# Token sums, norm transpose and placing between the first and second pair of a fused convolution and SwiGLU kernel: a change of places

## The chip, the cores and the metric

The kernel runs on one core of a Trainium2 chip. The metric is the device time of one execution in microseconds (us). The profiled execution was recorded by the hardware profiler; "the trace" is that record. Engines are named as the profile does: PE is TensorE (PEld its weight loads), DVE is VectorE, ACT is ScalarE, POOL is GpSimd, and SP is SyncE, which here only issues DMAs.

## The reference

A causal convolution over the tokens, with seven taps per head, is followed by a feed-forward block: RMS norm, two projections from 192 to 1536, SiLU of one times the other, and a projection back to 192. All is float32.

```python
# convolution: B=8, S=4096, D=192, 8 heads of 24 channels, K=7 taps
w = softmax(weight, axis=-1)
x_pad = concatenate([zeros(K - 1 tokens), x], axis=1)
x = einsum('hk,bskhg->bshg', w, x_unf)          # x_unf: windows of x_pad
# feed-forward: 32768 tokens, 192 -> 1536 -> 192
xn = x / sqrt(mean(x * x, axis=-1) + 1e-06) * rms_g
g, val = xn @ w_gate, xn @ w_val
out = (g * sigmoid(g) * val) @ w_out
```

## The kernel before

The 32768 tokens are cut into 32 "pairs" of 1024 tokens, each two groups of 512. A pair's normalised tokens lie channel by channel in the tile xb (two groups, three blocks of 64 channels; the lower 64 partitions serve the gate half, the upper 64 the value half).

**The first pair** is computed plainly: L1012 makes the projections, L1052 the output product (function outer, L1045). Its output product collects two token blocks in each of two PSUM banks, one for either half of the array. ScalarE copies the lower bank to o_sb (function low, L1060), then VectorE adds the upper bank to it (function upp, L1064) and so frees the upper bank. This happens four times: twice for each group of tokens. L1069 stores a finished group.

**All later pairs** use a scheme with fewer products: instead of eight products of blocks it makes seven, and pays with sums of blocks. For the input side those are the token sums (x_sum, L667 to L671, eleven for each pair, listed in XSUM at L67: target, and two operands, of which 0 to 5 are blocks of xb and 6 to 15 are earlier sums in the tile xc) and weight sums made once (w_sums, L342). Products (L760) add up in PSUM banks, and ScalarE and VectorE copy and add banks between them. For the output side the weight sums are made once by GpSimd (out_sums, L823 to L829, twelve small subtractions of L826), and the output products are L900.

There are eight banks, ps0 to ps7; the first four are for the lower half of the array, the others for the upper. The second pair's products run in a fixed order. The first two of them write ps2 and ps6, then ps1 and ps7 (the fourth product waits for the upp that frees ps7), then ps0 and ps4 (the sixth waits for the last upp, which frees ps4), then ps2 and ps6 again, then ps3 and ps5, which ScalarE fills with copies of ps1 and ps7 before.

**The work ahead.** While a pair is multiplied, the tokens of a pair two places later are convolved and normalised. The norm has five steps (norm, L512): square on ScalarE (L461), reduce on VectorE (L472 to L474), factor on GpSimd (L478, L481 and two copies L484: the power -1/2 and its spreading over heads), spread on VectorE (L491, a transpose), and scale on GpSimd (L499, 128x1536). place (L623) writes the result to DRAM through eight DMAs on SyncE's queue (L636), from where fetch reads it back channel by channel into xb. load (L154) brings raw tokens, also through SyncE's queue.

**What sets the order.** In the steady state a list written out by hand (ORDER, L90) does, from the second pair on. Up to there a queue of due times does: put(at, do) at L695 enters a call under a number, and emit (L698) makes the calls in the order of their numbers; equal numbers go in the order of entry. The numbers are in units of the planner, not in us, and only their order counts. Each engine executes what it is given in that order, and waits where its input or its buffer isn't ready. base is the number at which the first pair's output product begins, and c is base + 200. From function outer the four upp lie at base + 1763, base + 1988, base + 2888 and base + 3788 (one pair of output products is 37.5). All calls in this queue come before ORDER begins, so the second pair's first products follow the first pair's last output products directly.

In the code before, the third pair's norm (pair number 2 in the code, counted from 0) stands at L1200, its placing at L1201, the second pair's eleven token sums at L1202 to L1205, and out_sums at L1206:

- reduce: base + 1800; factor: base + 2510; spread: base + 2620; scale: base + 2640; place: base + 2650
- the first seven token sums: base + 1860 to base + 2490; the eighth (number 10 of XSUM): base + 2560; the last three (numbers 8, 9, 4): base + 2895, 2900, 2905
- out_sums: twelve steps, base + 2600, 2660, and so on in steps of 60

Of the kernel before, what the change touches and what calls it, by code (L numbers as in the profile page):

```python
# [19 lines left out]
def kernel(  # L20
# [310 lines left out]
    def part(at, m, n):  # L331
        return spare[:, at : at + m * n].rearrange("p (m n) -> p m n", m=m)
# [179 lines left out]
    def norm(p):  # L512
        for part in (square, reduce, factor, spread, scale):
            part(p)
            yield
# [107 lines left out]
    def place(p):  # L623

        if p >= PAIRS:
            return
        y = yn.pop(p)  # L630
        xd = scr[p] = dram.tile([D, PT], F32, name="xd")
        to = xd[:].rearrange("(h a) (b t) -> h b a t", a=GS, t=TB)
        for first in range(2) if p == 1 else (0,):
            q = nc.scalar if first else nc.sync
            for h in range(first, H, 2 if p == 1 else 1):
                q.dma_start(out=to[h], in_=y[h::H])  # L636
            yield
# [57 lines left out]
    def put(at, do):  # L695
        heapq.heappush(line, (at, next(tick), do))
# [480 lines left out]
    def later(it, *places):  # L1177
        for at in places:
            put(at, functools.partial(next, it, None))

    base = NU * SPAN
# [6 lines left out]
    c = base + 200  # L1188
# [8 lines left out]
            at = c + 250 + 100 * k + 50 * j if j < 2 else c + 960 + 80 * k  # L1197
            put(at, functools.partial(part_tap, 2, k, j))
    put(base + 3900, functools.partial(load, 3))
    later(norm(2), c + 1510, c + 1600, c + 2310, c + 2420, c + 2440)  # L1200
    later(place(2), c + 2450)  # L1201
    xat = [c + i for i in (1660, 1730, 2060, 2130, 2200, 2270, 2290)]  # L1202
    xat += [c + 2360] + [base + i for i in (2895, 2900, 2905)]
    for i, at in zip((0, 1, 7, 2, 3, 5, 6, 10, 8, 9, 4), xat):
        put(at, functools.partial(x_sum, i))  # L1205
    later(out_sums(), *[base + 2600 + 60 * i for i in range(4 * NM)])  # L1206
# [49 lines left out]
```

## Time and profile before

| | us |
|---|---|
| three runs | 2610.17, 2610.87, 2611.08 |
| median | 2610.87 |
| the profiled execution's own time | 2610.16 |
| its span in the trace | 2608.0 |
| last output product of the first pair (L1052) ends | 134.59 |
| first product of the second pair (L760) | 133.79 |
| second pair's output products (L900) begin | 194.01 |
| third pair's products (L760) begin | 221.45 |

The mean granted clock of TensorE is 0.997 of full speed. The span is the time from the first to the last recorded work; 2.2 us of the execution's time lie around it. In a timeline, one line is a group of like instructions on one engine: start and length in us, engine, line of the code, operation, output and input tiles (with buffer numbers left out), how many, and in brackets the idle time before and what ended it. A product of L760 is recorded as two matmuls on one half of the array (64 of 128 rows), so a pair's 120 products are 240 records; two products, one on either half, run side by side.

### The profile page before, as it was taken

How to read it: one execution, taken by the hardware profiler on the slowest of the kernel's cores; microseconds unless marked ns; L12 is line 12 of the kernel's file. 1: busy time of each engine (PE TensorE's matmuls, PEld its weight loads, DVE VectorE, ACT ScalarE, POOL GpSimd, SP SyncE). 2: the span in 40 equal slices, each digit the busy share in tenths (PEclk: the TensorE clock that was granted, in tenths of full speed). 3: DMA queues.
4: the chain of work that ended last, by engine and by line, in shares of the span. 5: the costliest groups of instructions: out<-in, count | busy, mean ns of one | idle time of the engine just before them, and what ended most of it. 6: DMA issues, size and time to landing. Idle time of an engine off the chain costs nothing.

```text
span 2608.0 us, 60632 instructions
## 1 busy us (share of the span) xinstructions
PE 2573.4 (99%) x23794; PEld 1760.1 (67%) x23794; DVE 2318.2 (89%) x3679; ACT 1545.5 (59%) x2812; POOL 2190.9 (84%) x1786
## 2 busy tenths in 40 slices
PE   6999999999999999999999999999999999999999
PEld 3766667666676666676676766666766666766666
DVE  8989989889989889998899898898898998988975
ACT  5365556765556655557655566555576555676554
POOL 3888889888898888898888988888988888988877
PEclk9999999999999999999999999999999999999999
DMA  6212331223322223313133222233132332122220
GB/s 144 57 33 56 63 54 41 54 42 63 63 44 50 44 52 63 57 41 59 33 63 63 46 48 44 51 63 63 38 56 34 62 63 53 42 52 44 50 44 13
DMA packets 512635, 137.35 MB, mean 53 GB/s; under 512 B 484317, under 2 KB 486877, under 8 KB 512222
## 3 DMA queue, kind: packets, MB, share of 16 engines
q1 hardware_dynamic: 509100, 132.80, 26.8%
q8 instruction: 186, 3.05, 0.5%
q10 hardware_dynamic: 3248, 0.69, 0.1%
q14 instruction: 101, 0.82, 0.1%
HBM read 83.87 MB, written 49.55 MB: 51 GB/s over the span
## 4 chain that ended last, share of the span: by engine, by line
PE 97%; DVE 1%; POOL 1%; DMA 0%; issue 0%; ACT 0%; SPq 0%; DVEq 0%; POOLq 0%; ACTq 0%
PE ps L760 62%; PE ps L900 33%; PE ps L1012 2%; POOL wf L350 1%; DMA x<-in_x_dram 0%; DVE y L406 0%; DVE y L394 0%; PE ps L595 0%; DVE xc L304 0%; ACT xb L615 0%; DVE xc L671 0%; DVE ht L1029 0%; POOL yn L499 0%; POOL wf L346 0%; DVE y L389 0%
## 5 line engine op out<-in xcount | busy, mean ns | idle before, releaser
L760 PE MATMUL ps<-xc,wf 64*128 64x512 f32 x4960 | 1219.0, 592 | 0.0
L760 PEld LDWEIGHTS ps<-xc,wf 64*128 64x128 f32 x4960 | 681.4, 187 | 378.8 <-issue 185.0
L760 PE MATMUL ps<-xb,wf 64*128 64x512 f32 x2480 | 683.0, 591 | 4.4 <-DVE o_sb L1064 4.4
L709 ACT ACTIVATE tile<-ps 128x512 f32<-128x512 f32 x678 | 391.2, 593 | 396.6 <-PE ps L760 303.0
L709 ACT ACTIVATE tls<-ps 128x512 f32<-128x512 f32 (+1 forms) x562 | 323.5, 589 | 437.4 <-PE ps L760 220.9
L812 POOL TENSOR_TENSOR ht<-ht,tile 128x512 f32<-128x512 f32 x329 | 419.1, 1275 | 148.3 <-ACT tile L805 65.6
L760 PEld LDWEIGHTS ps<-xb,wf 64*128 64x128 f32 x2480 | 354.8, 187 | 187.2 <-issue 96.2
L812 POOL TENSOR_TENSOR ht<-ht,tls 128x512 f32<-128x512 f32 x260 | 330.8, 1274 | 86.1 <-ACT tls L805 42.1
L709 ACT ACTIVATE ps<-ps 128x512 f32<-128x512 f32 (+1 forms) x589 | 336.1, 580 | 88.6 <-PE ps L900 32.5
L928 POOL TENSOR_TENSOR early<-ht 128x512 f32<-128x512 f32 x279 | 354.9, 1276 | 5.1 <-POOL ht L812 0.3
L445 DVE SCALAR_TENSOR_TENSOR ps<-xh,tp,ps 128x512 f32<-128x512 f32 x450 | 320.6, 749 | 2.7 <-ACT ps L437 0.5
L900 PE MATMUL ps<-ht,wo_sb 128*32 128x128 f32 (+2 forms) x5208 | 318.4, 380 | 0.0
L900 PEld LDWEIGHTS ps<-ht,wo_sb 128*32 128x32 f32 x5208 | 233.8, 110 | 81.8 <-POOL ht L812 23.5
L900 PE MATMUL ps<-ht,x 128*32 128x128 f32 (+2 forms) x4464 | 250.7, 379 | 0.0
L792 DVE TENSOR_TENSOR tile<-ps,tile 128x512 f32<-128x512 f32 x349 | 237.8, 684 | 10.2 <-PE ps L760 5.4
L928 POOL TENSOR_TENSOR ht<-ht 128x512 f32<-128x512 f32 x186 | 238.7, 1283 | 4.9
L792 DVE TENSOR_TENSOR ht<-ps,tile 128x512 f32<-128x512 f32 x328 | 223.0, 682 | 6.4 <-ACT tile L709 6.4
L900 PEld LDWEIGHTS ps<-ht,x 128*32 128x32 f32 x4464 | 184.6, 110 | 61.2
L805 ACT ACTIVATE tile<-tile 128x512 f32<-128x512 f32 x349 | 214.5, 625 | 0.2 <-DVE tile L792 0.2
L792 DVE TENSOR_TENSOR ht<-ps,tls 128x512 f32<-128x512 f32 x292 | 199.4, 683 | 6.8 <-ACT tls L709 3.6
L792 DVE TENSOR_TENSOR tls<-ps,tls 128x512 f32<-128x512 f32 x271 | 185.2, 684 | 16.6 <-PE ps L760 13.5
L900 PE MATMUL ps<-early,x 128*32 128x256 f32 (+2 forms) x3348 | 196.0, 379 | 0.0
(130 smaller groups left out, 3260.3 us busy)
## 6 DMA issues: line engine op xcount, KB each, us to landing
xb<-xd SPq DMA_DIRECT2D x120, 384.0 KB
xd<-yn SPq DMA_DIRECT2D x244, 96.0 KB
xh<-in_x_dram SPq DMA_DIRECT2D x192, 105.0 KB
out_dram<-o_sb SPq DMA_DIRECT2D x122, 96.0 KB
out_dram<-o_sb SPq DMA_DIRECT2D x62, 128.0 KB
xh<-in_x_dram SPq DMA_DIRECT2D x56, 98.4 KB
out_dram<-o_sb SPq DMA_DIRECT2D x122, 32.0 KB
ht<-in_moe_w_gate_dram SPq DMA_DIRECT2D x12, 192.0 KB
```

The lines of the kernel that those rows point to most:

```text
L350: nc.gpsimd.tensor_tensor(out=t[:, d, :], in0=t[:, a, :], in1=t[:, b, :], op=ALU.add if op == "add" else ALU.subtract,)
L445: nc.vector.scalar_tensor_tensor(out=dst, in0=xk, scalar=w, in1=at, op0=ALU.mult, op1=ALU.add)
L709: nc.scalar.activation(out=dst, in_=src, func=AF.Copy, scale=float(s))
L760: nc.tensor.matmul(out=self.new(v, h, True) if first else self.old(v, h), lhsT=wf[self.u][HALF[h], WAT[i], :], rhs=x_op(XOP[i])[HALF[h]], ...
L792: nc.vector.tensor_tensor(out=self.hv(v) if h else t[:], in0=self.old(v, h), in1=t[:], op=plus(s))
L805: nc.scalar.activation(out=t[:], in_=src[:], func=AF.Silu)
L812: engine[eng].tensor_tensor(out=self.hv(v), in0=src, in1=t[:], op=ALU.mult)
L900: nc.tensor.matmul(out=self.bank(b)[i * Q : (i + 1) * Q, at : at + n], lhsT=left, rhs=cols, start=fresh, stop=True, skip_group_check=True, ...
L928: engine[eng].tensor_tensor(out=dst, in0=a, in1=b, op=op)
L1012: nc.tensor.matmul(out=bank(h, bks[h])[:], lhsT=wf[u][HALF[h], k * NF + f, :], rhs=xb[HALF[h], g, k, :], start=(k == 0), stop=(k == KP - 1 ...
```

## The change

Only numbers in the queue change, in three lines near the end of the kernel. The last three token sums of the second pair, numbers 8, 9 and 4 of XSUM, go from base + 2895, 2900 and 2905 to c + 2370, 2380 and 2390, which is base + 2570, 2580 and 2590: directly behind number 10. The norm's spread goes from base + 2620 to base + 2895, its scale from base + 2640 to base + 2900, and place from base + 2650 to base + 2905: behind the third upp (base + 2888) and ahead of the fourth (base + 3788).

```diff
     put(base + 3900, functools.partial(load, 3))
-    later(norm(2), c + 1510, c + 1600, c + 2310, c + 2420, c + 2440)
-    later(place(2), c + 2450)
+    later(norm(2), c + 1510, c + 1600, c + 2310, base + 2895, base + 2900)
+    later(place(2), base + 2905)
     xat = [c + i for i in (1660, 1730, 2060, 2130, 2200, 2270, 2290)]
-    xat += [c + 2360] + [base + i for i in (2895, 2900, 2905)]
+    xat += [c + i for i in (2360, 2370, 2380, 2390)]
     for i, at in zip((0, 1, 7, 2, 3, 5, 6, 10, 8, 9, 4), xat):
         put(at, functools.partial(x_sum, i))
```

The built programs differ in the order of two engines. VectorE, from the eighth token sum on:

```
before: sum 10 | L491 transpose | L1064 upp (ps7) | sums 8, 9, 4 | L1064 upp (ps4) | L786 ...
after:  sum 10 | sums 8, 9, 4 | L1064 upp (ps7) | L491 transpose | L1064 upp (ps4) | L786 ...
```

GpSimd, from the norm's factor on:

```
before: L478, L481, L484 x2 | L826 x1 | L499 scale | L826 x11 | L812 ...
after:  L478, L481, L484 x2 | L826 x5 | L499 scale | L826 x7 | L812 ...
```

The instructions of TensorE, ScalarE and SyncE stand in the same order as before.

## Prediction

> **What bounds the kernel now.** I read the page's busy shares first, then the waits of TensorE, then the chain of waits in order of time, then the timelines of VectorE and GpSimd around the one place where the chain leaves TensorE.
>
> ```profile
> PE 2573.4 (99%) x23794; PEld 1760.1 (67%) x23794; DVE 2318.2 (89%) x3679; ACT 1545.5 (59%) x2812; POOL 2190.9 (84%) x1786
> ```
>
> TensorE is the bound. Its waits after the start are one wait:
>
> ```profile
> PE ps L760 <- DVE o_sb L1064: 4.4, 1, 4.4
> PE ps L1052 <- DVE ht L1029: 0.3, 1, 0.3
> ```
>
> The chain of waits in order of time (start, length, what) shows where that is, and that nothing later in the run interrupts TensorE:
>
> ```profile
> 140.72 0.48 DVE o_sb L1064
> 141.25 52.77 PE ps L760 x230
> 194.01 27.44 PE ps L900 x337
> 221.45 51.92 PE ps L760 x240
> ```
>
> The third pair's 240 product records take 51.92 us (0.2163 each). The second pair's run from 133.79 (first product in TensorE's timeline) to 194.01, 60.22 us. So the handover from the first pair to the second loses 60.22 - 51.92 = 8.30 us, once. Everything after 194.01 repeats at a fixed length, so what is won here stays won.
>
> VectorE at the handover (start, length, form; the idle time before in brackets):
>
> ```profile
> 131.97 0.69 DVE L671 TENSOR_TENSOR xc<-xc 128x512 f32<-128x512 f32 x1
> 134.92 0.25 DVE L491 STREAM_TRANSPOSE s<-s 128x64 f32<-128x64 f32 x1 [2.26 <-POOL s L484]
> 135.09 0.52 DVE L1064 TENSOR_TENSOR o_sb<-ps,o_sb 128x384 f32<-128x384 f32 x1
> 135.54 4.19 DVE L671 TENSOR_TENSOR xc<-xb 128x512 f32<-128x512 f32 x2
> 139.65 1.07 DVE L671 TENSOR_TENSOR xc<-xb,xc 128x512 f32<-128x512 f32 x1
> 140.65 0.54 DVE L1064 TENSOR_TENSOR o_sb<-ps,o_sb 128x384 f32<-128x384 f32 x1
> ```
>
> GpSimd at the same time:
>
> ```profile
> 132.80 1.68 POOL L481 TENSOR_TENSOR r<-r,nhalf 128x8 f32<-128x8 f32 x1
> 134.54 0.35 POOL L484 COPY s<-r 128x32 f32<-128x32 f32 x2
> 134.85 0.59 POOL L826 TENSOR_TENSOR x<-wo_sb 128x192 f32<-128x192 f32 x1
> 135.41 2.82 POOL L499 TENSOR_TENSOR yn<-y,s 128x1536 f32<-128x1536 f32 x1
> 138.15 2.03 POOL L826 TENSOR_TENSOR x<-wo_sb 128x192 f32<-128x192 f32 x2
> ```
>
> VectorE idles 2.26 us for the norm's transpose (L491), then sums the first bank (L1064 at 135.09, which TensorE's fourth product needs), then makes three token sums. The last of L1064, at 140.65, frees the bank that the sixth product writes, and stands behind all three. The first two of these sums took 4.19 us because the third pair's multiply (L499) ran beside them. TensorE stopped from 136.87 to 141.25, 4.38 us. The stop has a second bill, seen in the table by stretches (us, then busy time of PE, PEld, DVE, ACT, POOL; granted clock; DMA):
>
> ```profile
> 141.25:147.06 5.81, 5.81 (x14) 2.49 (x16) 2.77 (x5) 0.89 (x2) 4.29 (x8) 0.53 0.79 177
> 147.06:194.01 46.95, 46.95 (x222) 35.56 (x222) 42.27 (x68) 38.65 (x72) 36.17 (x29) 1.00 0.14 17
> ```
>
> For 5.81 us after the stop the clock is 0.53: 14 records in 5.81 us, which need 14 x 0.2163 = 3.03 at full clock, so 2.78 us are lost. The 8.30 are thus 4.38 stop, 2.78 slow clock, and 1.14 small waits: 0.73 for the first L1064, the rest the overlap with the last output products and ScalarE's copies.
>
> [...] 4.19 for two sums beside L499 against 0.69 for the one at 131.97. [...] clock 0.50 from 140.0, after 3.1 us of idleness, until about 146.7. [...] the trace has one of 1.1 us (before the first product of the kernel, at 38.61) with the clock at 1.00 after it.
>
> **The change part by part.** No instruction is added or removed; VectorE's and GpSimd's orders change at one place each, those of TensorE, ScalarE and SyncE don't. The new VectorE order behind the sum at 131.97 is: three token sums, first L1064, transpose, second L1064. On GpSimd four more of the weight sums (L826) go ahead of L499.
>
> *The three sums* now start at 132.66, in the time in which VectorE idled. What runs beside them is the norm's small work, L478, L481, L484. The steady state shows this very pairing:
>
> ```profile
> 218.83 1.47 DVE L671 TENSOR_TENSOR xc<-xc 128x512 f32<-128x512 f32 x2
> 219.05 1.96 POOL L481 TENSOR_TENSOR r<-r,nhalf 128x8 f32<-128x8 f32 x1
> ```
>
> Two sums in 1.47 us, so L481 doesn't hold VectorE, and itself stretches from 1.68 to 1.96. Of the three sums two read xb twice; that form took 0.94 to 0.96 at 125.77 and 129.44 beside GpSimd's small weight sums. Two by 0.96 and one by 0.75 is 2.67: they end at 132.66 + 2.67 = 135.33. Bounds: 3 x 0.69 = 2.07 below; above, 2.1 each as beside L499, 6.3. I take 2.67, because L499 itself can't run beside them: it needs the transpose, which is now behind them.
>
> *First L1064*: ready since its ScalarE half at 125.54, it runs at 135.33 to 135.85. Before it ended at 135.61, so the fourth product comes 0.24 late, at about 135.9 instead of 135.67.
>
> *Transpose*: GpSimd's factors are done at 134.89 + 0.28 (stretched L481) = 135.17, so at 135.8 it waits for nothing: 135.8 to 136.05. The 2.26 us of idleness are gone.
>
> *Second L1064*: its ScalarE half ended at 133.82, TensorE's last output product at about 134.6. It runs 136.0 to 136.55 instead of 140.65 to 141.19. The sixth product follows the fourth in the same half of the array, one product (0.86) later: 135.9 + 0.86 = 136.8. The bank is free before that, so the stop of 4.38 is gone, and with it the slow clock.
>
> *What is late next*: the ninth product writes a bank that ScalarE fills by its second copy after the fourth product. ScalarE starts when that ends, 136.8 plus the 0.04 to 0.3 seen, takes 1.07 for two, so about 138.1. In the steady state that product starts 3.46 us (four steps of 0.865) after the first. Counted back from 138.1 to 138.5 (the ninth and tenth) the second pair stands as if started undisturbed at 134.6 to 135.0. Before it stands as if started at 194.01 - 51.92 = 142.09. Gain 142.09 - 135.0 = 7.1 us, of 8.30 at most.
>
> *The moved multiply, L499*: GpSimd does five L826 from 135.17 (0.57 each without the sums beside them) to 138.0, L499 to 140.9, seven L826 to about 144.9. Before it was through at 145.53. Its next work, the first L812, came at 152.65 after 7.12 of idleness; drawn 7.1 ahead it is due at 145.5. Cover 0.6 us, so I cost it at nothing; if GpSimd is 1 us late, at most some tenths reach TensorE, through tiles that come free late. VectorE beside L499 then does PSUM work with one SBUF input, which it does in every later pair too (L499 at 306.46 beside L776 of 0.70 us).
>
> *The moved placing, L636*: eight DMAs start at 140.9 instead of 138.25, and take 5.23 on SyncE's queue; the store (L1069) behind them goes from 143.59 to about 146.2, the eight loads of the fourth pair (7.20 us) from 144.18 to 146.8, done about 154. First readers: the fetch at 193.83 and ScalarE's tap at 193.00, drawn ahead to about 186. Over 30 us of cover: nothing.
>
> Sum: -7.1 us. On the profiled execution's own time, 2610.16, that is 2603.1; on the median of 2610.87, 2603.8. The profiled execution is the lowest of all, so I take 2603.6.
>
> **The rivals.**
> 1. *The sums stay slow in their new place.* [...] At 1.7 us each (the usual length beside L928-type work at 209.91 is 1.77), the first L1064 ends at 138.3, the fourth product waits 3.5 us instead of 1, the pair stands as started at 137.5, and the slow clock may or may not come: 4.6 gained without it, 1.8 with it: 2606.3 to 2609.1. Against it: the pairing at 218.83.
> 2. *GpSimd becomes the bound of the first products.* If all twelve L826 take the 1.03 seen beside sums, it is through at 135.2 + 12.4 + 2.9 = 150.5, 5 us late for the first L812. If all of it reached TensorE, 2.1 are left: 2608.8; half of it, 2606.3. For it: the order puts four L826 ahead of L499. Against it: the 1.03 were seen only while sums ran, and none run there.
> 3. *The other sign: the starved sums hold both banks.* [...] now the first L1064 is behind them too, so that TensorE stops two products earlier. With the 3.20 that is the longest sum in the trace each, the sums end at 142.3, the fourth product starts at 142.9, the pair stands as started at 142.0, and with 2.8 of slow clock at 144.8, against 142.09: 2.7 slower, 2613.6. It decides from 2.3 us a sum (132.66 + 6.9 + 0.6 - 0.87 + 2.8 = 142.09). Being over 0.2% slower would need some 4 us a sum.
>
> That the change doesn't do what it says is excluded by the two orders, which show the moves.
>
> **How the numbers follow.** 0.2% is 5.2 us, about what a measurement of this kernel tells from no change, so faster means under 2605.7. My forecast has 0.84, rival 1 0.07 (no change), rival 2 0.05 (half of it faster), rival 3 0.04 (three quarters of it slower by over 0.2%, as whatever starves VectorE so long would hold up its next work too; the rest no change). Within my case the sum length (2.07 to 3.1) and ScalarE's copies give 6.0 to 8.2 us gained: 2602.4 to 2604.9. The range reaches a little into rivals 1 and 2: 2602.2 to 2606.4. Faster 0.84 + 0.025, about 0.86; same 0.07 + 0.025 + 0.01, about 0.11; slower 0.03.
>
> **What would show it.** Right: no wait of TensorE on L1064 over 1 us; clock at 1.00 through 135 to 150; the three sums from 132.7 to about 135.3; L491 without idle time before it; the second pair's L760 ending near 187. Wrong: sums of over 1.2 us beside L484 or L826; a clock of 0.5 anywhere near 140; an idle TensorE released by GpSimd L812 or ScalarE L709 in the first 20 us of the second pair.

## The result, and the profile after

The kernel after takes 2603.47 us (median of 8 runs, 2602.35 to 2603.79), the kernel before 2610.68 us in the same comparison (2610.04 to 2611.89): 7.2 us less, a ratio of 0.9971 (95% interval 0.996 to 0.9982). The forecast was 2603.6.

The chain of waits after, in order of time (start, length, what):

```profile
119.96 14.62 PE ps L1052 x175
134.58 0.16 PE ps L760
134.74 0.32 PE ps L1052 x2
135.07 51.66 PE ps L760 x238
186.73 27.44 PE ps L900 x337
214.17 51.92 PE ps L760 x240
```

It stays on TensorE through the whole handover from the first to the second pair, where before it went over VectorE and GpSimd. From 186.73 on the lengths are those of before (27.44 and 51.92), only earlier.

The first product comes a little earlier or later in each execution (133.79 to 135.19 in the profiles here), so below I measure the **handover**: from the first L760 of the second pair to its first L900 in the chain. Before it is 194.01 - 133.79 = 60.22 us. After, the first L760 stands at 134.26:

```profile
134.26 0.69 PE L760 MATMUL ps<-xc,wf 64*128 64x512 f32 x1
```

The handover is thus 186.73 - 134.26 = 52.47. Undisturbed it would be 51.92. So 7.75 of the 8.30 us are gone, and 0.55 is left. What follows the first L900 is the same everywhere: 2413.8 to 2414.2 us of the span in all eleven profiles, so start and handover together make up the differences.

TensorE's waits after (total, times, longest) (those after the start) have no line with L1064 any more:

```profile
PE ps L1012 <- ACT xb L615: 1.1, 1, 1.1
PE ps L1052 <- DVE ht L1029: 0.3, 1, 0.3
```

VectorE's timeline after:

```profile
132.63 0.69 DVE L671 TENSOR_TENSOR xc<-xc 128x512 f32<-128x512 f32 x1
133.24 1.29 DVE L671 TENSOR_TENSOR xc<-xb 128x512 f32<-128x512 f32 x2
134.46 0.68 DVE L671 TENSOR_TENSOR xc<-xb,xc 128x512 f32<-128x512 f32 x1
135.06 0.55 DVE L1064 TENSOR_TENSOR o_sb<-ps,o_sb 128x384 f32<-128x384 f32 x1
135.91 0.24 DVE L491 STREAM_TRANSPOSE s<-s 128x64 f32<-128x64 f32 x1 [0.31 <-POOL s L484]
136.08 0.52 DVE L1064 TENSOR_TENSOR o_sb<-ps,o_sb 128x384 f32<-128x384 f32 x1
```

The two sums that took 4.19 us take 1.29, and all three lie where VectorE idled. The 4.19 were not two sums slowed alike. The timeline of before, ended at 138.6, shows the first of them alone:

```profile
135.54 3.20 DVE L671 TENSOR_TENSOR xc<-xb 128x512 f32<-128x512 f32 x1
```

It ends at 138.74, 0.51 us after GpSimd's multiply (L499, 135.41 to 138.23); the second and third took 1.07 each beside GpSimd's weight sums. So a single sum lost about 2.5 us beside the multiply (3.20 against 0.69 for the sum at 131.97).

The second bank sum runs 1.8 us after the first product instead of 6.9. GpSimd's timeline after:

```profile
133.46 2.00 POOL L481 TENSOR_TENSOR r<-r,nhalf 128x8 f32<-128x8 f32 x1
135.52 0.35 POOL L484 COPY s<-r 128x32 f32<-128x32 f32 x2
...
138.57 2.89 POOL L499 TENSOR_TENSOR yn<-y,s 128x1536 f32<-128x1536 f32 x1
...
143.52 1.71 POOL L826 TENSOR_TENSOR x<-wo_sb,x 128x192 f32<-128x192 f32 x3
145.35 1.27 POOL L812 TENSOR_TENSOR ht<-ht,tile 128x512 f32<-128x512 f32 x1
```

The multiply L499 has moved behind the bank sums, and the first L812 follows the weight sums without a pause. The table by stretches (us, then busy time of PE, PEld, DVE, ACT, POOL; granted clock; DMA share, GB/s) shows the clock:

```profile
136.00:139.00 3.00, 3.00 (x16) 1.62 (x14) 2.29 (x5) 2.23 (x5) 3.00 (x6) 1.00 0.00 0
139.00:142.00 3.00, 3.00 (x18) 1.33 (x16) 2.90 (x6) 1.78 (x4) 3.00 (x3) 1.00 0.00 0
142.00:147.00 5.00, 5.00 (x26) 2.72 (x24) 4.32 (x7) 3.21 (x7) 4.50 (x7) 1.00 0.57 126
```

TensorE is busy throughout and the clock is 1.00, where before it was 0.53 for 5.81 us.

### The profile page after: what moved, and what is told of

It is laid out like the page before. It is cut to its first block, busy times and chain, and to the rows that moved or that the text cites. A ratio compares the mean times of both kernels' runs of the same rounds, so it can differ in the third digit from the quotient of the medians.

```text
span 2600.6 us, 60632 instructions
## 1 busy us (share of the span) xinstructions
PE 2570.1 (99%) x23794; PEld 1757.2 (68%) x23794; DVE 2312.1 (89%) x3679; ACT 1546.1 (59%) x2812; POOL 2192.4 (84%) x1786
## 4 chain that ended last, share of the span: by engine, by line
PE 96%; DVE 2%; DMA 1%; SPq 1%; issue 0%; DVEq 0%; POOL 0%; POOLq 0%
PE ps L760 62%; PE ps L900 33%; PE ps L1052 1%; DMA xh<-in_x_dram 0%; DMA ht<-in_moe_w_val_dram 0%; DMA x<-in_x_dram 0%; SPq L217 0%; SPq L1149 0%; DVE ht L1029 0%; DVE y L421 0%; DVE wf L319 0%; SPq L144 0%; DVE xc L304 0%; DVE xc L287 0%; DVE xc L294 0%
## 5 line engine op out<-in xcount | busy, mean ns | idle before, releaser
L760 PE MATMUL ps<-xc,wf 64*128 64x512 f32 x4960 | 1214.4, 591 | 0.0
L760 PEld LDWEIGHTS ps<-xc,wf 64*128 64x128 f32 x4960 | 679.3, 186 | 377.4 <-issue 183.8
L760 PE MATMUL ps<-xb,wf 64*128 64x512 f32 x2480 | 680.5, 591 | 0.0
L812 POOL TENSOR_TENSOR ht<-ht,tile 128x512 f32<-128x512 f32 x329 | 419.8, 1278 | 140.3 <-ACT tile L805 64.9
L760 PEld LDWEIGHTS ps<-xb,wf 64*128 64x128 f32 x2480 | 353.6, 187 | 183.2 <-issue 96.5
L812 POOL TENSOR_TENSOR ht<-ht,tls 128x512 f32<-128x512 f32 x260 | 331.5, 1278 | 85.4 <-ACT tls L805 41.2
L900 PE MATMUL ps<-ht,wo_sb 128*32 128x128 f32 (+2 forms) x5208 | 318.5, 380 | 0.0
L900 PEld LDWEIGHTS ps<-ht,wo_sb 128*32 128x32 f32 x5208 | 233.8, 110 | 81.7 <-POOL ht L812 23.5
L900 PE MATMUL ps<-ht,x 128*32 128x128 f32 (+2 forms) x4464 | 250.7, 379 | 0.0
L900 PEld LDWEIGHTS ps<-ht,x 128*32 128x32 f32 x4464 | 184.5, 110 | 61.2
L900 PE MATMUL ps<-early,x 128*32 128x256 f32 (+2 forms) x3348 | 196.0, 379 | 0.0
```

What stands on the lines that cost most here:

```text
L760: nc.tensor.matmul(out=self.new(v, h, True) if first else self.old(v, h), lhsT=wf[self.u][HALF[h], WAT[i], :], rhs=x_op(XOP[i])[HALF[h]], ...
L812: engine[eng].tensor_tensor(out=self.hv(v), in0=src, in1=t[:], op=ALU.mult)
L900: nc.tensor.matmul(out=self.bank(b)[i * Q : (i + 1) * Q, at : at + n], lhsT=left, rhs=cols, start=fresh, stop=True, skip_group_check=True, ...
```

## The experiments

All change only this handover. Theory A was that the token sums between the two bank sums were the cost, with the collision (token sums beside GpSimd's multiply L499) and the slow clock on top. The expectations set a rival theory, B to E, against it each time. All times are compared with the kernel before in the same session. "Stop" is the longest idle time of TensorE in the handover; two values are two profiles of the same program.

| run | handover, us | stop of TensorE, us | slow clock | median, us | ratio to before (95%) |
|---|---|---|---|---|---|
| before | 60.22 | 4.38 | yes | 2610.5 to 2610.8 | |
| after | 52.47 | none | no | 2603.47 | 0.9971 (0.996 to 0.9982) |
| sums only | 53.31 | 0.41 | no | 2604.27 | 0.9975 (0.9964 to 0.9985) |
| norm only | 54.96, 56.55 | 2.05, 1.93 | no, yes | 2606.16 | 0.9982 (0.9976 to 0.9989) |
| multiply only | 57.03, 57.09 | 2.18, 2.19 | yes, yes | 2607.05 | 0.9986 (0.998 to 0.9993) |
| two sums more | 54.10 | 1.20 | no | 2604.87 | 0.9978 (0.9969 to 0.9987) |
| six sums more | 62.13 | 7.63 | yes | 2612.75 | 1.0007 (0.9999 to 1.0016) |
| kept busy | 57.39 | filled | no | 2608.18 | 0.999 (0.9983 to 0.9997) |
| banks first | 52.32 | none | no | 2602.38 | 0.9969 (0.9957 to 0.998) |

**Sums only.**

```diff
-    xat += [c + 2360] + [base + i for i in (2895, 2900, 2905)]
+    xat += [c + i for i in (2360, 2370, 2380, 2390)]
```

> Only the three token sums move; transpose, multiply and placing stay as before. Theory A (the sums were the cost, the norm's move only spares a small wait): the sums take about 0.6 us each as in the kernel after, the transpose then waits for GpSimd until about 135.9 and the first bank sum stands behind it, so the fourth product comes about 1 us later than after. No stop over 2 us, clock at 1.00, handover (first product of the second pair to its first output product) about 53.4 us against 60.2 before and 52.5 after; about 6.3 us faster than before. Theory B (the collision with the norm's multiply was the cost, so that moving that is what counts): most of the gain is missing, handover 58 us or more.

Handover 53.31, and 6.5 us faster than before by the medians, as theory A had it; theory B asked for a handover of 58 or more. VectorE's timeline:

```profile
134.17 1.29 DVE L671 TENSOR_TENSOR xc<-xb 128x512 f32<-128x512 f32 x2
135.38 0.68 DVE L671 TENSOR_TENSOR xc<-xb,xc 128x512 f32<-128x512 f32 x1
136.84 0.25 DVE L491 STREAM_TRANSPOSE s<-s 128x64 f32<-128x64 f32 x1 [0.78 <-POOL s L484]
137.01 0.98 DVE L1064 TENSOR_TENSOR o_sb<-ps,o_sb 128x384 f32<-128x384 f32 x2
```

The transpose waits 0.78 us for GpSimd, and the first bank sum behind it: it starts 1.82 us after the first product (137.01 against 135.19), after the whole change 0.80. So the sums alone bring 6.91 of the 7.75. Moving the norm's steps as well is worth the other 0.84, by these two profiles, and the transpose ahead of the first bank sum is what the timeline shows of it; the medians (0.8 apart) have overlapping intervals.

**Norm only.**

```diff
-    later(norm(2), c + 1510, c + 1600, c + 2310, c + 2420, c + 2440)
-    later(place(2), c + 2450)
+    later(norm(2), c + 1510, c + 1600, c + 2310, base + 2895, base + 2900)
+    later(place(2), base + 2905)
```

> Only transpose, multiply and placing move behind the first bank sum; the three token sums stay between the two bank sums. Theory A: the sums still hold the second bank. They run from about 135.1 beside GpSimd's small weight sums at about 1.05 us each, second bank sum done at about 138.8, TensorE stops for about 3 us[...]: handover 55.2 us without it, 58 with it (5.0 or 2.2 us faster than before). Theory B: as the multiply no longer runs beside the sums, nearly the whole gain is there, handover under 53.5 us.

The timelines of VectorE and TensorE:

```profile
135.88 0.25 DVE L491 STREAM_TRANSPOSE s<-s 128x64 f32<-128x64 f32 x1 [1.80 <-POOL s L484]
136.04 1.89 DVE L671 TENSOR_TENSOR xc<-xb 128x512 f32<-128x512 f32 x2
137.86 1.07 DVE L671 TENSOR_TENSOR xc<-xb,xc 128x512 f32<-128x512 f32 x1
138.85 0.55 DVE L1064 TENSOR_TENSOR o_sb<-ps,o_sb 128x384 f32<-128x384 f32 x1
```

```profile
139.45 0.69 PE L760 MATMUL ps<-xb,wf 64*128 64x512 f32 x1 [2.05 <-DVE o_sb L1064]
```

The sums still stand before the second bank sum and still hold it, now all beside the weight sums at about 1 us each, without the one of 3.20 beside L499. The stop is 2.05 us, where I expected about 3. Handover 54.96, close to the 55.2 expected without the slow clock (58 was for the case with it), and 2.49 worse than with both parts moved: theory B, under which it should be under 53.5, falls. But the collision was real money too, since this part alone brings 5.26 (4.6 by the medians). The two parts' gains can't be added: either one takes away most of the stop, and in these two profiles the slow clock with it.

**Multiply only.** VectorE's order is that of before; L499 and the placing stand behind four more weight sums.

```diff
-    later(norm(2), c + 1510, c + 1600, c + 2310, c + 2420, c + 2440)
-    later(place(2), c + 2450)
+    later(norm(2), c + 1510, c + 1600, c + 2310, c + 2420, base + 2900)
+    later(place(2), base + 2905)
```

> VectorE's order is that of before; only the multiply and the placing move behind four more weight sums on GpSimd. This prices the collision alone. Theory A: two sums of 4.19 us become 2.1 (beside weight sums, 1.05 each), the second bank sum ends at about 139.1, TensorE stops for about 2.3 us and the clock stays at 1.00: 4.8 us faster, of which 2.8 are the clock, handover about 55.4. Theory C (the weight sums hold VectorE as much as the multiply does): sums of 1.7 to 2.1 us each, stop over 4 us, slow clock, no gain.

VectorE's two sums and the clock in the table by stretches:

```profile
135.66 2.00 DVE L671 TENSOR_TENSOR xc<-xb 128x512 f32<-128x512 f32 x2
```

```profile
139.18:143.03 3.85, 3.85 (x10) 1.68 (x12) 1.70 (x3) 0.60 (x1) 3.85 (x4) 0.56 0.00 0
143.03:190.94 47.91, 47.91 (x226) 35.99 (x226) 43.35 (x70) 38.96 (x72) 38.82 (x34) 1.00 0.25 43
```

With L499 out of the way, the two sums' 4.19 us become 2.00 (both now beside weight sums) and the stop 4.38 becomes 2.18, as theory A had it; theory C (sums as slow beside weight sums as beside L499) falls. My expectation was wrong on the clock: it halved even after this shorter stop, for one stretch that ended at about 143.0, and the handover is 57.03 instead of 55.4.

**Two and six sums more.** In the kernel after, the last token sum is made again, with the same inputs, between the transpose and the second bank sum; six times in the one run, in the other with range(2):

```diff
         put(at, functools.partial(x_sum, i))
+    for _ in range(6):
+        put(base + 2897, functools.partial(x_sum, 4))
```

> The kernel after with the last token sum made six times more (same inputs, same result) between the transpose and the second bank sum. Theory A: the sums run at 1 us beside the weight sums and at 2 us beside the multiply, some 7 to 9 us together; TensorE stops for 6 to 8 us and the clock halves: cost against after is the stop plus 2.8, 9 to 11 us, so 2 to 4 us slower than before. Theory D (the slow clock costs nothing of its own): cost is the stop alone, 6 to 8 us, no slower than before.

> The kernel after with the last token sum made two times more between the transpose and the second bank sum. Theory A: 0.97 us each beside the weight sums, as in the run with six more; the sixth product comes 1.95 us later than after, a stop of about 1.7 us, and the handover is 54.4 us if so short a stop leaves the clock alone (2 us slower than after), 56.1 if one window of 3.4 us at half clock follows, as in the run with only the multiply moved, whose stop was 2.2 us.

The lines of the run with six, from VectorE's timeline, TensorE's, and the table by stretches:

```profile
136.65 8.06 DVE L671 TENSOR_TENSOR xc<-xb,xc 128x512 f32<-128x512 f32 x6
144.63 0.55 DVE L1064 TENSOR_TENSOR o_sb<-ps,o_sb 128x384 f32<-128x384 f32 x1
```

```profile
145.23 1.22 PE L760 MATMUL ps<-xb,wf 64*128 64x512 f32 x1 [7.63 <-DVE o_sb L1064]
```

```profile
145.23:148.50 3.27, 3.27 (x8) 1.51 (x10) 1.24 (x2) 0.60 (x1) 3.20 (x6) 0.50 0.64 142
```

The sixth product comes 10.47 us after the first (145.23 against 134.76) where after it comes at 2.39 (136.65 against 134.26): 8.08 later, which is the 8.06 of the sums. Five of the six sums took about 1 us each beside weight sums, the last 3.16 beside L499. The handover is 9.66 longer than after; the rest, 1.58, is the slow clock, half of the 3.27 us. My expectation had 2.8 for it: more than half of the slow time fell into the stop itself, where it costs nothing. With two more sums (1.89 us) the sixth product comes 1.65 us later, the handover is 1.63 longer, and the clock stays at 1.00. So what stands between the two bank sums is paid nearly or fully on TensorE, and after the long stop the clock is paid besides. Theory D (no bill for the clock) falls for the run with six by its slow stretch; the times alone (2612.75 against 2610.76, interval up to 1.0016) are weaker.

**Kept busy.** In the kernel before, the fifth product of the second pair is made five more times into the same bank, started anew each time (again is a list of five entries, set up further above):

```diff
                 start=first, stop=True, skip_group_check=True,
             )
+            while again and (v, h, i) == (5, 0, 6):
+                again.pop()
+                nc.tensor.matmul(
+                    out=self.old(v, h), lhsT=wf[self.u][HALF[h], WAT[i], :],
+                    rhs=x_op(XOP[i])[HALF[h]], start=True, stop=True, skip_group_check=True,
+                )
```

> The kernel before, with the fifth product of the second pair (bank ps0) made five more times in TensorE's order, each time anew with the same result. They fill the stop of 4.38 us with work on one half of the array and change no other engine's order. Theory A (the slow clock is a bill of its own, raised by idleness): clock 1.00 throughout, the sixth product still comes at about 141.3, handover (first product of the second pair to its first output product) about 57.4 us against 60.2, 2.8 us faster than before. Theory D (the half clock has another cause, or half an array doesn't count as busy): handover about 60.2, time as before.

TensorE's timeline and the stretches (the added product's line is L769, the products' L762 in this kernel):

```profile
137.28 4.45 PE L769 MATMUL ps<-xb,wf 64*128 64x512 f32 x10
141.83 0.69 PE L762 MATMUL ps<-xb,wf 64*128 64x512 f32 x1
```

and, from its chain of waits, the way from the sixth product to the first output product:

```profile
141.83 50.07 PE ps L762 x230
```

```profile
141.83:147.60 5.77, 5.77 (x28) 2.71 (x29) 5.03 (x8) 2.82 (x5) 4.32 (x8) 1.00 0.81 180
```

The sixth product comes 7.32 us after the first, as before (7.46), so the wait itself is untouched. But 28 records instead of 14 run in the next 5.8 us, the clock is 1.00, and the handover is 57.39, 2.83 shorter. Of that, 2.70 is the clock's: from the sixth product on it takes 50.07 us, before 52.77 (and after 50.08). The rest is the slightly earlier sixth product. The prediction had put 2.78 down to the clock. Theory D falls here too. Work on one half of the array was enough to keep the clock up: ten records from 137.28 to 141.83, with the clock at 1.00 in that stretch too. The kernel is 2.3 us faster than before (0.9983 to 0.9997) for doing more.

**Banks first.** A version to beat both: first bank sum, token sums, second bank sum, transpose; multiply and placing last.

```diff
-    later(norm(2), c + 1510, c + 1600, c + 2310, base + 2895, base + 2900)
-    later(place(2), base + 2905)
+    later(norm(2), c + 1510, c + 1600, c + 2310, base + 3795, base + 3796)
+    later(place(2), base + 3797)
-    xat += [c + i for i in (2360, 2370, 2380, 2390)]
+    xat += [c + 2360] + [base + i for i in (2889, 2890, 2891)]
```

> VectorE's order: first bank sum, the three token sums, second bank sum, transpose; multiply and placing behind all weight sums. The fourth product waits for nothing now. The sums end at about 135.6, the second bank sum at about 136.1. Theory A: TensorE loses only the overlap with the last output products; handover 52.1 to 52.4 us against 52.5 after, which the times can't tell from after (within 0.5 us). Theory E (GpSimd becomes the bound, as its first multiply of the second pair now comes behind everything): handover 53 us or more.

Handover 52.32 against 52.47; theory E asked for 53 or more and falls. The fourth product starts 1.50 us after the first in both kernels. The 0.15 comes from the sixth: it starts 2.36 us after the first instead of 2.39, its second record 2.79 instead of 2.92. Its median is 1.1 us under that of after, but the intervals nearly coincide; it isn't shown to be faster.

**Norm only and multiply only, profiled once more**, for what makes the clock fall.

> The kernel with only the multiply and placing moved, profiled once more. The first profile has one window of 3.4 us at half clock after a stop of 2.2 us; the kernel with the norm moved has a stop of 2.1 us and no slow clock. If the length of the stop decides, the slow clock comes again, handover 57.0. If it is where the stop falls in a window that isn't tied to the kernel, this profile may show none, handover 55.3.

> The kernel with the norm moved and the sums left, profiled once more. If the length of the stop decides, no slow clock again, handover 55.0. If it is where the stop falls in the window, a slow clock of 3.4 us may come, handover 56.7.

"Multiply only" had its slow stretch again, handover 57.09. "Norm only", which had none, now had one, after a stop that was shorter than the first time. TensorE's line and the stretch:

```profile
138.59 0.69 PE L760 MATMUL ps<-xb,wf 64*128 64x512 f32 x1 [1.93 <-DVE o_sb L1064]
```

```profile
138.59:142.81 4.22, 4.22 (x12) 1.88 (x14) 2.44 (x4) 0.60 (x1) 4.22 (x4) 0.60 0.00 0
```

In the first profile 20 records ran in the 4.22 us after the stop, here 12. Handover 56.55 instead of 54.96. So the length of the stop alone doesn't decide at about 2 us: 1.93 brought the slow clock, 2.05 did not, and both are of the same program.

The traces' record of the clock tells more. The times between two changes of the clock are 3.413 us or whole multiples of it in all eleven traces (before, 6.827 is two of them, 105.81 is 31). So in these traces the clock changed only on a grid of steps of 3.413 us, and the grid lies differently in each execution (the clock falls at 139.65 in the first profile of "multiply only", at 141.47 in the second). Carried on from the changes at the kernel's start, it gives the following steps around the stop, first for the second profile of "norm only", then for the first. The figure after the comma is TensorE's busy time, so the first step has 3.41 - 1.48 = 1.93 us of idleness:

```profile
136.02:139.43 3.41, 1.48 (x7) 0.49 (x6) 3.11 (x5) 1.16 (x3) 3.41 (x5) 1.00 0.00 0
139.43:142.84 3.41, 3.41 (x10) 1.39 (x8) 1.92 (x3) 0.60 (x1) 3.41 (x3) 0.50 0.00 0
```

```profile
134.47:137.89 3.42, 2.93 (x16) 1.70 (x14) 2.02 (x4) 2.04 (x5) 3.36 (x6) 1.00 0.02 5
137.89:141.30 3.41, 1.85 (x10) 0.91 (x12) 2.72 (x5) 0.89 (x2) 3.41 (x4) 1.00 0.00 0
141.30:144.71 3.41, 3.41 (x19) 1.53 (x17) 3.21 (x7) 1.71 (x4) 3.41 (x5) 1.00 0.13 28
```

The stop of 1.93 us lies whole in one step, and the clock is halved in the next. The stop of 2.05 is cut into 0.49 and 1.56, and the clock stays. All eleven handovers fit: the clock fell after steps with 1.93, 2.18, 2.19, 3.04 and 3.41 us of idleness, and after none with 1.56 or less. An edge near 1.9 is my estimate from these steps, since one step with 1.93 early in the second profile of "norm only" (23.38 to 26.79) brought no fall. The clock came back after a step in which TensorE was busy but for at most 0.16 us (with six sums more, from 145.07 to the restart at 145.23). Before, the step after the fall still had 1.34 us of the stop in it, so the clock stayed low for two steps instead of one. This is what these eleven traces show; no run placed a stop on the grid on purpose.

## Why the prediction was right

The mechanism, its place and its size came out, point by point:

- *The stop and its bill.* Both terms of the 8.30 us were measured by themselves: the wait, which grows by the length of what is put before the second bank sum (8.06 us of sums, 8.08 later), and the slow clock (2.70 by the run kept busy, against 2.78 worked out from the count of records). Of the rest, 1.14, the prediction gave 0.73 to the first bank sum. That was too much: before, the fourth product starts 1.88 us after the first (135.67 against 133.79), and in "banks first", where nothing holds it, 1.50 after.
- *The three sums.* This is the term that was mis-sized. I took 2.67 us, with 0.96 for each sum of two blocks of xb, from the lines at 125.77 and 129.44. They took 1.82 us from the first's start to the first bank sum (133.24 to 135.06), about 0.6 each. The 0.96 had GpSimd's weight sums beside it; L481 beside the new place didn't hold VectorE. I had used the line at 218.83 for just that, and should have taken its 0.73 for all three. So such a sum ran longer beside L499 (3.20) and beside the weight sums (0.94 to 1.07), but not beside L481 (about 0.6). What makes the difference, no run shows.
- *The collision.* The prediction read the 4.19 us as "2.1 each as beside L499". They are one sum of 3.20 beside it and one of 1.07 behind it. The forecast does not rest on this, since the sums leave L499 behind, but the upper bound of 6.3 us for three and rival 3's three times 3.20 do: a single L499 held up a single sum, as in the run with six.
- *First bank sum and fourth product.* The product was forecast at 2.1 us after the first. The bank sum was done 1.34 us after it (135.60 against 134.26), and the product started at 1.50 (135.77), no later than in "banks first": it was not held at all. The bank sum came sooner by the 0.85 that the sums saved, less 0.1 because they began that much later against the first product.
- *Transpose.* Forecast without a wait; it waits 0.31 us for L484, because the sums were done 0.7 us sooner against the first product and L484 0.2 later. L481 stretched to 2.00 as taken from the steady state (1.96). The second bank sum was ready before its product all the same.
- *What is late next.* ScalarE's copies for the ninth product: forecast to be done 4.3 us after the first product, done at 3.6 (136.82 + 1.07 = 137.89). That leaves a handover of 52.47 instead of the 53.1 forecast.
- *GpSimd.* Forecast through at 144.9 with the first L812 due at 145.5; it was through at 145.23, and L812 began at 145.35. It precedes the first L900 by 41.38 us, before by 41.36: no time was lost. The cover that I put at 0.6 us was all used, though. Rival 2 was near.
- *SyncE.* Placing at 141.49, store at 146.84, loads from 147.44 (forecast 140.9, 146.2, 146.8), first readers at 185.72 and 186.54: nothing, as forecast.
- *The sum.* -7.1 forecast, -7.75 in the handover. The first product came 0.47 us later in the profiled execution of after than in that of before, and the spans are 7.4 apart; the medians 7.2. The interval of the ratio (4.7 to 10.4 us) holds both figures. That 2603.6 comes within 0.2 us of the measured 2603.47 is in part luck. The handover gave 0.65 more than forecast, and the start, which no term of the forecast has, took 0.47 back in the profiled execution; it differs by 1.0 us between two profiles of one program (133.91 and 134.93).

Rivals 1 and 3 needed sums of 1.7 and over 2.3 us; they took 0.6. What rival 3 feared needs more work ahead of the bank than this change puts there: with six more sums ahead of the second bank sum, the kernel is as slow as before or slower.

## What to carry to other kernels

On an engine that works in order (before, VectorE idled 2.26 us at L491, ahead of a bank sum that in "banks first" ran without a wait, at 132.92), look at what stands between an instruction whose input is ready and the bank that it frees: nearly all of it is paid on the engine that waits for the bank (8.08 us for 8.06, 1.65 for 1.89). Work that is ready early belongs into the idle time ahead of a wait, not behind it (the three sums alone brought 6.91 us), and a big multiply on GpSimd belongs where VectorE doesn't add two SBUF tiles (here one such sum took 3.20 us instead of 0.69). A stop of TensorE of about 2 us cost a second time through the clock (1.93 us, 1.7 us more), or not (2.05 us), by where the clock's steps of 3.413 us cut it. From about 4 us on it would wherever they lie, an estimate: twice the 1.9 to 2 of idleness that sufficed in one step. So count the records in the stretch after a stop, not the idle time alone.

## What the runs showed of the hardware

- The clock halved after a stop of only 1.93 us (second profile of "norm only"), and did so after the restart: the slow stretch began 0.84 us after TensorE had gone on, 138.59 to 139.43. After the stop of 2.05 us in the first profile it stayed at 1.00. In the traces the changes of the clock lie 3.413 us or whole multiples of it apart (before, 6.827 and 105.81).
- The slow stretches of the handovers lasted one step ("multiply only": 139.65 to 143.06) or two (before, 139.90 to 146.73; six sums more, 141.66 to 148.48). Their bill in the handover was 2.70 us before, 1.7 in "multiply only" and in the second profile of "norm only", and 1.6 with six sums more.
- Useless products on one half of the array kept the clock at 1.00 through a wait of 4.4 us, and made the whole kernel 2.3 us faster.
- A token sum of two blocks in SBUF took 0.6 us start to start beside L481 (a power of 128x8; 1.29 for two in after), and about 1 us beside small subtractions of 128x192 (2.00 for two in "multiply only"). A sum that ran beside the 128x1536 multiply took 3.20 us before and 3.16 with six sums more.
